# Attention and a two-stage mixer on one core: transfers turn q, k and x, more seven-product pairs, V's products on quarter row tiles

## The chip, the cores and the metric

The kernel runs on one core of a Trainium2 chip. TensorE (PE in the profile) multiplies, VectorE (DVE), ScalarE (ACT) and GpSimd (POOL) work on elements, SyncE (SP) only issues transfers, as POOL does too; 16 DMA engines carry them. The metric is the device time of one execution in microseconds; lower is better.

## What is computed

```python
def attention(q, k, v):                       # 4 x 8 heads x 768 x 64, n_global 8, n_local 96
    scores = q @ k.T / 8                      # a key is kept if it is one of the first 8,
    scores += -slope[h] * distance            # or lies 0 to 95 places behind the query
    return softmax(where(keep, scores, -1e9)) @ v
def mixer(x):                                 # x: 4 x 768 x 512, the heads side by side
    u = x + (x.T @ U @ V).T                   # U 768 x 32, V 32 x 768: low rank over the sequence
    return u + maximum(u @ w_ch1, 0) @ w_ch2  # 512 -> 2048 -> 512
```

The matrix products take fp16 and add in fp32.

## The kernel before, in words

**Pairs.** The 4 batches x 8 heads are handled as 16 pairs of heads, numbered 0 to 15; pairs 4b to 4b+3 are batch b. For each pair POOL loads q, k and v (`lq`, `lk`, `lv`), casting them to fp16; SP loads q and k of pair 0. The head size has to be on the partitions for q times k, so PE turns q and k by multiplying with the identity, six 128 x 128 pieces a turn for pairs from 4 on (`TQ`, `TK`, L611), and ACT or DVE copies the result out of PSUM (`EQ`, `EK`). `KO` builds a shifted copy of k whose first 32 keys are the global ones, `VC` and `VG` the same for v. `S` forms the scores (L734, 64 rows of the array a head, so two products run side by side), `EX` takes the exponential on ACT, `MK` multiplies by the mask, `PV` multiplies with v (L866, L867), and `RC` and `NM` divide and write x in fp32.

**The low rank.** `XC` casts x to fp16. `UP` sends six pieces of it through PE twice: times the identity, which leaves x turned in PSUM (L840), and times U (L845). `XE` copies the 32 columns of x U out, four times side by side, `XU` turns them (L948), `TE` copies them to `tmp`, and `HM` multiplies with V (L966) on top of the turned x in PSUM: the result is u turned. `HM` has two products of 384 columns; where `HR` says R, they take 64 rows each (32 with numbers and 32 of zeros, half a `vs` tile) and run side by side, for pairs 1, 8 and 12 they take all 128 rows. `E0` copies u from PSUM to `uT`, mostly on ACT.

**First layer of the mixer**, per batch: 16 tiles of 128 columns of w_ch1. A plain tile is `M1` (L1020, L1044: eight products of 384 columns) and a ReLU on ACT. Two tiles, j and j + 8, can instead be formed together by seven block products (Winograd's form of Strassen's scheme): `ZP1` to `ZP7` (L1115), each two products of 384 columns, 14 in place of 16. `ZT` forms the sums of u for it, `ZS` those of the weights; ACT keeps three partial sums (`ZU`, `ZW`, `ZX`), DVE adds them to PSUM (`ZA`, `ZB`, `ZD`, L1133), and separate ReLU passes follow over the results (`ZQ`, `ZV`, L1172, L1174). 14 pairs of tiles are done so: four each in batches 1 and 2, six in batch 3.

**Second layer**, per batch three units t, each 128 + 128 rows of the output, again by seven products `P1` to `P7` of eight products of 256 columns (L1246), with sums formed by `PA` and `PB`. `RS` adds the low-rank part through V (L1238, four products of 256 columns, 64 rows each), `DA` to `DH` add PSUM onto x, and `O` stores.

**The order.** `ORDER` lists some 1,000 tasks by short names, and a planner in the program assigns buffers and PSUM banks from booked durations and due times. Each engine then runs its tasks strictly in the list's order; each waits by semaphore for what it needs. A batch's attention is woven between the products of the batch before. q and k have three staging buffers, v four, turned q and k three each, x in fp16 three.

Of the kernel before, what the change touches and what calls it, by code (L numbers as in the profile page):

```python
# [10 lines left out]
FP32 = mybir.dt.float32  # L11
FP16 = mybir.dt.float16
# [9 lines left out]
wz iota lk1 lk0 lq0 vz relf bias1 rel3 bias0 lq1 lk3 bias2 bias4 Ck0.1 ones0 lv0 Ck0.0 SB0.2 vs1 mask1 Cq0.0 Cq0.1  # L22
SB0.0 TK0 lk2 EK0.0 EK0.1 KO0.1 lq2 KO0.0 TQ0 EQ0.0 lq3 EQ0.1 mask2 SB0.1 ones1 TK1 EK1 back S0.0 S0.2 S0.1 lv1 TQ1
EQ1 KO1 VC0 VG0 ones2 ones3 lk4 EX0.0 EX0.1 u16 TK3 EK3 EX0.2 SB1.1 SB1.2 S1.2 EX1.2 S1.1 EX1.1 vs0 PV0 RC0 NM0 XC0
KO3 lv2 TK2 EK2 KO2 VC1 VG1 lk5 SB2.1 TQ2 EQ2 SB1.0 S1.0 EX1.0 lv3 SB2.2 lq4 lq5 TQ3 S2.2 EX2.2 EQ3 S2.1 mixl PV1
SB3.1 S3.1 RC1 NM1 UP0 XE0 XC1 w1_1 EX2.1 w1_5 SB2.0 EX3.1 S2.0 XU0 TE0 VC2 SB3.0 TK4 EK4 VG2 HM0 S3.0 TK5 EK5 VC3
VG3 EX2.0 E00 SB3.2 w1_7 S3.2 w1_6 PV2 RC2 NM2 UP1 XC2 EX3.0 TQ4 EX3.2 lk7 PV3.0 PV3.1 PV3.2 RC3.2 XE1 XU1 RC3.0
NH3.0 RC3.1 NH3.1 lq7 NH3.2 NM3 EQ4 KO4 TE1 TQ5 EQ5 UP2 XE2 HM1 E01 UP3.0 XU2 TE2 UP3.1 UP3.2 XE3 HM2 E02 XU3 TE3
M1a0.3 M1c0.3 HM3 E03 vs2 E13 KO5 S4.1 lv4 EX4.1 mask0 EX4.2 M1d0.3 M1b0.3 RL0.3 M1a0.14 M1b0.14 w1_4 RL0.14 M1b0.15
lq6 M1b0.13 RM0.13 M1a0.2 M1c0.2 TK7 M1d0.2 MK4.1 RM0.15 w1_2 MK4.2 VC4 M1a0.13 VG4 RM0.14 EK7 KO7 RL0.13 M1b0.2  # L30
RL0.2 ZS6 w1_0 M1a0.15 S4.0 EX4.0 MK4.0 S5.0 w1_3 EX5.0 M1a0.10 mask3 TQ7 EQ7 lk6 mask5 M1a0.11 TQ6 EQ6 RL0.15
RL0.11 PV4 RC4 M1b0.4 RL0.10 lv5 M1b0.11 RM0.4 NM4 XC4 w2_2 w2_0 RM0.11 M1b0.12 S5.1 EX5.1 w2_3 ZS5 RM0.12 M1a0.6
M1b0.10 M1a0.12 EX5.2 w2_1 RM0.10 M1b0.7 RM0.7 TK6 EK6 KO6 M1a0.8 M1a0.0 RL0.6 ZS7 RL0.12 M1c0.0 M1d0.0 M1b0.0 RL0.0
lk8 MK5.0 MK5.1 VC5 TD0 VG5 MK5.2 PV5 M1a0.4 RL0.4 M1a0.7 PA0.3 PB0.3 UP4 XE4 RL0.7 M1a0.5 lq8 RL0.8 RC5 NM5 XC5
M1b0.5 RM0.5 M1b0.6 RM0.6 M1b0.8 RM0.8 RL0.5 XU4 TE4 TWa0 lk9 lv7 TWb0 PA0.1 PB0.1 M1a0.1 M1c0.1 M1d0.1 M1b0.1 RL0.1
PA0.0 PB0.0 M1b0.9 M1a0.9 S7.0 lk10 RM0.9 RL0.9 PA0.2 PB0.2 EX7.0 HM4 E04 RS0.0 P20.0 P10.0 DA0.0 lq9 mask7 TWa1
TWb1 S6.1 EX6.1 EX6.2 RS0.1 P10.1 P20.1 DA0.1 mask6 lv6 TQ8 P30.1 DF0.1 TK8 lq10 MK7.0 EQ8 UP5 XE5 VC7 P50.0 lq12
VG7 EK8 XU5 TE5 lk11 mask4 P30.0 DF0.0 S6.0 EX6.0 HM5 E05 MK6.2 P60.0 DB0.0 MK6.1 P60.1 DB0.1 S7.1 MK6.0 EX7.2 RS0.2
MK7.2 P10.2 DA0.2 P70.1 DD0.1 TQ10 lq11 EX7.1 MK7.1 TK9 EK9 KO9 ZS4 P70.0 lv11 TQ9 P20.2 EQ10 VC11 VC6 VG6 EQ9 TK10
EK10 KO10 DD0.0 P40.1 DG0.1 PV7 RC7 NM7 PV6 KO8 RC6 NM6 lv8 P60.2 P30.2 DC0.0 XC7 DB0.2 P50.1 DC0.1 XC6 UP7 UP6 XE7  # L40
DF0.2 P40.0 DG0.0 lv10 XE6 XU6 TE6 XU7 TE7 lv9 P70.2 DD0.2 HM6 E06 HM7 E07 S8.0 EX8.0 lq14 E17 ZP11.5 MK8.0 ZU1.5
P40.2 S8.1 EX8.2 EX8.1 TK11 EK11 ZT1 ZP11.4 ZU1.4 P50.2 M1a1.3 TQ11 M1b1.3 RL1.3 ZP21.5 ZP61.5 ZW1.5 O0.3 ZP21.4
DG0.2 KO11 EQ11 ZA1.5 ZA1.4 DC0.2 ZP61.4 ZW1.4 S9.1 EX9.1 MK8.1 ZP71.5 ZX1.5 M1a1.6 RL1.6 MK9.1 VC10 ZP71.4 ZX1.4
ZP51.5 ZB1.5 O0.4 M1a1.7 ZP51.4 VC9 EX9.2 ZB1.4 ZV1.4 ZP11.6 ZP31.5 ZP41.5 ZD1.5 ZR1.5 ZP41.4 ZP31.4 MK8.2 O0.2
ZD1.4 M1a1.2 M1b1.2 ZP11.7 ZR1.4 ZQ1.5 ZV1.5 ZQ1.4 PA1.2 O0.0 PB1.2 M1b1.6 ZU1.6 ZP61.6 RL1.7 ZU1.7 ZP21.7 ZA1.7
RL1.2 VC8 ZP61.7 ZW1.7 RM1.6 ZW1.6 M1a1.4 ZP21.6 ZA1.6 O0.5 VG8 PV8 ZP71.7 RL1.4 ZP71.6 ZX1.6 RC8 lk13 M1b1.7 RM1.7
O0.1 NM8 XC8 ZX1.7 PA1.1 S9.0 EX9.0 M1b1.5 M1b1.4 RM1.4 ZP51.6 ZB1.6 ZP41.6 RM1.5 UP8 XE8 MK9.0 ZP51.7 lk12 ZR1.6
TK12 EK12 TD1 ZP31.6 ZB1.7 M1a1.5 ZV1.7 ZD1.6 TQ12 RL1.5 XU8 EQ12 TE8 ZP41.7 ZR1.7 lv12 ZP31.7 ZD1.7 M1a1.0 M1b1.0
HM8 M1a1.1 M1b1.1 MK9.2 ZV1.6 RL1.0 ZQ1.6 ZQ1.7 PA1.3 PB1.1 E08 RL1.1 PA1.0 VG9 PV9 S10.1 RC9 RS1.1 P11.1 P21.1 lv14
P51.1 EX10.2 NM9 S10.0 PB1.3 PB1.0 DA1.1 EX10.1 XC9 S11.0 EX11.0 MK11.0 EX10.0 RS1.0 P21.0 P51.0 DC1.0 S11.1 EX11.2  # L50
P31.0 P11.0 MK10.1 P31.1 UP9 DF1.0 TQ14 VC12 EX11.1 DA1.0 P61.0 XE9 XU9 KO12 EQ14 TE9 MK11.2 MK11.1 VG11 PV11 lk14
TK14 lk15 EK14 DB1.0 P71.0 O1.0 DF1.1 P61.1 lq13 RC11 NM11 MK10.2 DD1.0 XC11 HM9 E09 S12.0 EX12.0 RS1.2 P11.2 P41.0
KO14 S12.1 EX12.1 DB1.1 P71.1 VG12 EX12.2 P31.2 DA1.2 MK10.0 VG10 DD1.1 PV10 MK12.0 TK13 EK13 P61.2 lq15 RC10 TQ13
EQ13 NM10 P21.2 XC10 KO13 UP10 lv13 UP11 XE10 DB1.2 P71.2 XU10 DF1.2 DC1.1 DG1.0 TE10 DD1.2 XE11 XU11 TE11 P41.1
DG1.1 VC14 O1.4 O1.3 HM10 E010 S14.0 EX14.0 HM11 E111 E011 MK12.1 MK14.0 P41.2 ZP12.7 ZU2.7 S14.1 EX14.2 ZT2 MK14.2
EX14.1 M1a2.5 ZP12.6 P51.2 DC1.2 M1a2.1 M1b2.1 TK15 EK15 KO15 ZU2.6 DG1.2 ZP62.6 RL2.5 ZP62.7 ZW2.6 M1b2.4 RL2.1
ZP72.6 ZX2.6 ZP52.6 ZB2.6 ZP12.4 RM2.4 M1a2.4 RL2.4 ZP22.7 ZA2.7 TQ15 EQ15 ZP32.6 ZD2.6 M1b2.5 ZP42.6 RM2.5 MK12.2
ZR2.6 M1a2.3 TD2 M1b2.3 PV12 ZP22.6 ZW2.7 ZP72.7 MK14.1 RL2.3 RC12 ZX2.7 ZP52.7 O1.2 M1a2.0 M1b2.0 O1.5 O1.1 NM12
XC12 ZB2.7 ZP32.7 ZU2.4 ZA2.6 ZQ2.6 ZV2.7 ZV2.6 VG14 PV14 RL2.0 ZD2.7 ZP62.4 ZP12.5 RC14 NM14 ZW2.4 ZP42.7 ZP22.4
ZA2.4 ZU2.5 ZR2.7 UP12 XE12 ZP72.4 PA2.0 ZX2.4 M1a2.7 ZP62.5 ZW2.5 ZP22.5 ZA2.5 XU12 TE12 ZP52.4 ZP42.4 RL2.7 ZP72.5  # L60
ZP52.5 HM12 M1a2.2 ZB2.4 ZX2.5 ZR2.4 ZB2.5 ZV2.5 M1b2.2 E012 ZP32.5 ZP42.5 ZR2.5 M1b2.7 RM2.7 XC14 UP14 XE14 ZP32.4
M1b2.6 ZQ2.7 PA2.3 ZD2.5 ZQ2.5 RL2.2 ZV2.4 ZD2.4 ZQ2.4 PA2.2 PB2.2 XU14 TE14 RM2.6 M1a2.6 RL2.6 PB2.0 PA2.1 RS2.1
HM14 E014 RS2.0 P12.0 DA2.0 P22.0 S13.1 EX13.1 EX13.2 P22.1 P12.1 P52.1 P62.0 S15.1 PB2.1 PB2.3 P32.0 EX15.2 MK13.1
DA2.1 DB2.0 P32.1 P62.1 P72.0 MK13.2 EX15.1 DF2.1 DF2.0 MK15.1 S13.0 EX13.0 lv15 S15.0 RS2.2 MK15.2 P52.2 P12.2
MK13.0 VG13 VC13 PV13 EX15.0 DB2.1 P72.1 MK15.0 DD2.0 VC15 RC13 VG15 PV15 DA2.2 NM13 RC15 P42.0 NM15 P62.2 ZS3.2
DD2.1 XC13 P22.2 UP13 XC15 UP15 DB2.2 P72.2 XE15 XU15 TE15 DG2.0 XE13 XU13 TE13 P32.2 DD2.2 HM13 HM15 E015 E115
DF2.2 ZS3.3 P52.0 P42.1 E013 ZP13.5 ZU3.5 M1a3.0 M1b3.0 ZT3 ZP13.2 RL3.0 DG2.1 DC2.1 O2.1 P42.2 ZP13.4 ZU3.2 ZP63.5
M1a3.1 ZU3.4 DC2.0 ZW3.5 ZP63.4 ZP73.5 DG2.2 ZW3.4 DC2.2 O2.5 ZX3.5 ZP63.2 ZP53.5 M1b3.1 ZB3.5 ZW3.2 RL3.1 ZP23.5
ZA3.5 ZP43.5 ZP73.4 ZV3.5 ZP23.4 ZA3.4 ZX3.4 ZP73.2 ZX3.2 ZP13.3 ZU3.3 TD3 ZR3.5 ZP53.4 ZB3.4 ZP33.5 ZD3.5 ZQ3.5
ZP43.4 ZR3.4 ZV3.4 ZP13.7 ZU3.7 ZP23.3 ZA3.3 ZP63.3 ZP33.4 ZD3.4 ZP53.2 ZB3.2 M1a3.5 ZW3.3 O2.3 ZQ3.4 PA3.2 RL3.5  # L70
O2.4 ZP43.2 ZR3.2 ZP23.2 ZA3.2 ZP13.6 ZU3.6 ZP53.3 ZP63.7 ZW3.7 ZP23.6 ZA3.6 ZP63.6 ZW3.6 ZP73.3 ZX3.3 ZP53.6 ZP73.7
ZX3.7 ZB3.3 ZP53.7 ZV3.2 ZB3.7 ZV3.7 ZP73.6 ZX3.6 ZP43.3 ZR3.3 ZP43.7 ZB3.6 M1b3.4 RM3.4 ZP33.7 ZD3.7 ZP43.6 ZP33.6
ZP33.2 ZD3.6 ZR3.6 ZV3.6 ZQ3.6 ZP33.3 ZR3.7 ZD3.3 ZV3.3 O2.0 M1a3.4 RL3.4 M1b3.5 RM3.5 ZP23.7 ZD3.2 ZA3.7 ZQ3.7
PA3.3 RS3.1 RS3.0 RS3.2 P23.2 ZQ3.3 ZQ3.2 PA3.1 P23.0 P23.1 P13.0 P13.2 PA3.0 PB3.0 P53.1 DA3.0 DA3.2 P13.1 P63.2
P53.0 PB3.3 O2.2 DA3.1 P63.0 DB3.2 PB3.2 P63.1 P53.2 PB3.1 P33.0 DB3.0 P73.0 DC3.1 DB3.1 P33.1 DF3.2 DC3.0 P33.2
O3.2a DC3.2 DF3.1 P73.1 O3.1 P73.2 DH3.2 O3.2 DD3.0 P43.0 DF3.0 O3.0 DD3.1 P43.1 DD3.2 P43.2a P43.2b O3.5a DG3.0
# [9 lines left out]
class Task:  # L86
    def __init__(self, name, eng, dur, fn, deps=(), lat=0.1, acq=(), rel=(), size=0.0, parts=1, mode=0, bw=(), br=(), fast=0):
        self.name, self.eng, self.dur, self.fn = name, eng, dur, fn
        self.deps = [d for d in deps if d is not None]
        self.lat, self.fast = lat, fast  # L90
        self.acq, self.rel, self.size, self.parts, self.mode = acq, rel, size, parts, mode
        self.start = self.end = None

        self.bw, self.br = bw, tuple(br) + tuple(g for g in rel if g.kind == "ps" and eng != PE)
# [11 lines left out]
class Planner:  # L106


    LANES = 8

    def __init__(self, counts, dma_rate, switch):
        self.tasks, self.names = [], {}
# [147 lines left out]
def kernel(  # L260
# [13 lines left out]
    nc = tc.nc  # L274
# [1124 lines left out]
```

## Time and profile before

| | |
|---|---|
| Time, median of 3 runs (lowest, highest) | 225.12 us (224.36, 225.25) |
| Span of the profiled execution, first to last instruction | 223.0 us |
| What lies around it, median less span | 2.1 us |
| PE busy, of the span | 216.4 us, 97% |
| DVE, ACT, POOL busy | 181.6, 147.0, 73.7 us |
| Products on PE (matmul instructions) | 2,424 |
| SP's transfers, issue (least, median, most) and landing | 0.585, 0.616, 2.116 us for the vo copies; 2.5 us to landing for 124 KB |

The profiled execution's own time is the span and about 2.1 us around it. "Busy" on PE counts a product from its start to its modelled end; products overlap, so the price of one in a row of products is the distance between starts. In the chain of waits a piece such as "0.34 PE ps L611 x6" is six products that took 0.34 us of PE's queue.

### The profile page before, as it was taken

Reading aid. Unit: us, or ns where it says so; the run is one execution under the profiler, and the core shown is the slowest. Engines: PE = TensorE matmul, PEld = TensorE weight load, DVE = VectorE, ACT = ScalarE, POOL = GpSimd, SP = SyncE. Lnnn points to the kernel's source line nnn. Section 1 sums busy time; section 2 is a strip of 40 time slices with the busy share of each in tenths; the row PEclk is TensorE's granted clock in tenths of the full one; section 3 lists DMA queues with packets and bytes.
Section 4 is the critical chain, followed back from the end, with each engine's and each line's share of the span. In section 5 each row is a group of like instructions: output and inputs, shape, how many; then the busy total and the mean of one; then the engine's idle time right before and its main releaser. Section 6 shows DMA issues by size and latency. Waiting matters only on the chain.

```text
span 223.0 us, 5965 instructions
## 1 busy us (share of the span) xinstructions
PE 216.4 (97%) x2424; PEld 158.5 (71%) x2424; DVE 181.6 (81%) x403; ACT 147.0 (66%) x260; POOL 73.7 (33%) x97
## 2 busy tenths in 40 slices
PE   8799899999999999999999999999999999999994
PEld 3466656675879976666888876666788875658883
DVE  5688966999987987888978688597978796889872
ACT  7888798768858669788757557787742458782000
POOL 8989959714894940010851000011000000000000
PEclk9999999999999999999999999999999999999999
DMA  6999999999999997662997021409100006000025
GB/s 173 178 170 149 159 161 185 184 206 166 158 157 92 140 191 141 224 46 37 68 116 98 18 79 65 132 4 71 33 0 3 0 3 259 25 1 3 0 97 190
DMA packets 87404, 23.31 MB, mean 104 GB/s; under 512 B 73840, under 2 KB 84784, under 8 KB 87376
## 3 DMA queue, kind: packets, MB, share of 16 engines
q0 software_dynamic: 72880, 13.74, 75.6%
q1 hardware_dynamic: 14496, 9.19, 14.2%
q8 instruction: 19, 0.31, 0.6%
q14 instruction: 9, 0.07, 0.1%
HBM read 27.56 MB, written 6.29 MB: 152 GB/s over the span
## 4 chain that ended last, share of the span: by engine, by line
PE 84%; DMA 7%; POOL 5%; issue 2%; DVE 1%; ACT 0%; DVEq 0%; POOLq 0%
PE ps L1246 34%; PE ps L1115 14%; PE ps L1020 11%; PE ps L1044 7%; PE ps L734 4%; DMA vt<-in_v_dram 4%; PE ps L611 3%; DMA stgq<-in_q_dram 3%; PE ps L840 2%; PE ps L867 2%; PE ps L866 2%; POOL stgq L457 1%; POOL w L507 1%; PE ps L1238 1%; PE ps L966 1%
## 5 line engine op out<-in xcount | busy, mean ns | idle before, releaser
L799 ACT ACTIVATE ep<-ps 128x1024 f16<-128x1024 f32 (+1 forms) x48 | 44.0, 952 | 16.3 <-PE ps L734 15.1
L1246 PEld LDWEIGHTS <-htr 128*128 128x128 f16 x392 | 36.2, 98 | 6.1 <-issue 1.9
L1020 PE MATMUL ps<-uT,w 128*128 128x384 f16 x176 | 33.3, 326 | 0.0
L1258 DVE TENSOR_TENSOR x_sb<-x_sb,ps 128x256 f32<-128x256 f32 (+1 forms) x60 | 26.8, 463 | 7.6 <-PE ps L1246 7.2
L1246 PEld LDWEIGHTS <-sA 128*128 128x128 f16 x288 | 27.4, 98 | 4.2 <-issue 0.7
L461 POOL DMA_DIRECT2D vt<-in_v_dram x16 | 16.7, 1047 | 32.9 <-PE ps L867 29.7
L1026 ACT ACTIVATE htr<-ps 128x384 f16<-128x384 f32 x44 | 20.7, 493 | 5.6 <-PE ps L1020 5.3
L1246 PE MATMUL ps<-w,sA 128*128 128x256 f16 x192 | 24.2, 273 | 0.0
L1246 PE MATMUL ps<-tB,htr 128*128 128x256 f16 (+1 forms) x200 | 24.2, 268 | 0.0
L1020 PEld LDWEIGHTS <-w 128*128 128x128 f16 x176 | 16.5, 98 | 10.6
L1246 PE MATMUL ps<-w,htr 128*128 128x256 f16 x192 | 23.5, 273 | 0.0
L457 POOL DMA_DIRECT2D stgq<-in_q_dram x24 | 19.9, 852 | 5.4 <-PE ps L611 3.3
L1044 PE MATMUL ps<-uT,w 128*128 128x384 f16 x112 | 21.3, 326 | 0.0
L457 POOL DMA_DIRECT2D stgk<-in_k_dram x24 | 20.0, 852 | 2.6 <-DMA w<-in_moe_w_ch_dram 1.0
L1133 DVE TENSOR_TENSOR htr<-ps,zu 128x384 f16<-128x384 f32 x30 | 16.4, 553 | 4.7 <-PE ps L1115 3.0
L362 ACT ACTIVATE zu<-ps 128x384 f32<-128x384 f32 x30 | 14.7, 493 | 5.7 <-PE ps L1115 5.3
L812 DVE TENSOR_TENSOR ep<-ep,mask 128x1024 f16<-128x1024 f16 x24 | 16.2, 684 | 1.4 <-ACT ep L799 0.9
L905 DVE TENSOR_TENSOR x_sb<-ps,rcp 128x768 f32<-128x768 f32 x16 | 15.3, 956 | 0.9 <-DMA vo<-vt 0.4
L1044 PEld LDWEIGHTS <-w 128*128 128x128 f16 x112 | 10.7, 98 | 6.6
L1115 PEld LDWEIGHTS <-w 128*128 128x128 f16 x108 | 10.2, 98 | 6.1
L734 PE MATMUL ps<-qT,kT 64*128 64x128 f16 x192 | 14.0, 217 | 0.4 <-DVE kT L364 0.4
L1115 PE MATMUL ps<-uT,w 128*128 128x384 f16 x56 | 13.4, 326 | 0.0
(124 smaller groups left out, 450.0 us busy)
## 6 DMA issues: line engine op xcount, KB each, us to landing
out_dram<-x_sb SPq DMA_DIRECT2D x20, 256.0 KB, 2.2
vt<-in_v_dram POOLq DMA_DIRECT2D x16, 192.0 KB, 5.9
stgk<-in_k_dram POOLq DMA_DIRECT2D x24, 96.0 KB, 6.6
stgq<-in_q_dram POOLq DMA_DIRECT2D x24, 96.0 KB, 5.6
w<-in_moe_w_ch_dram POOLq DMA_DIRECT2D x8, 256.0 KB, 7.1
w<-in_moe_w_ch_dram POOLq DMA_DIRECT2D x4, 512.0 KB, 11.7
vo<-vt SPq DMA_DIRECT2D x8, 123.8 KB, 2.5
out_dram<-x_sb SPq DMA_DIRECT2D x7, 128.0 KB, 2.2
```

The lines of the kernel that those rows point to most:

```text
L457: nc.gpsimd.dma_start(o[:, i], src[b, h0 + i].rearrange("(n p) d -> p n d", p=P))
L461: nc.gpsimd.dma_start(vt[gv.slot][:, :, :, 0:D], v[b, h0:h0 + 2].rearrange("h (n p) d -> p h n d", p=P),)
L734: nc.tensor.matmul(t[:, hi, j * P:(j + 1) * P], lhs, qt[r, i * P:(i + 1) * P], start=not biased, stop=True, skip_group_check=biased,)
L799: nc.scalar.activation(ep[gep.slot][:, :, lo:512], ps[:, gsc.slot:gsc.slot + 2, lo:512], AF.Exp, scale=qk_scale)
L812: nc.vector.tensor_tensor(ev, ev, mv, ALU.mult)
L1020: nc.tensor.matmul(ps[:, g.slot, 0:HS], w1[:, dc, jt * P:(jt + 1) * P], ub[:, dc, i * HS:(i + 1) * HS], start=(dc == 0), stop=(dc == NDC - 1),
L1026: nc.scalar.activation(htr[:, jt, i * HS:(i + 1) * HS], ps[:, g.slot, 0:HS], AF.Relu)
L1044: nc.tensor.matmul(ps[:, g.slot + half, 0:HS], w1[:, dc, jt * P:(jt + 1) * P], ub[:, dc, half * HS:(half + 1) * HS], start=(dc == flat[0]) ...
L1115: nc.tensor.matmul(bank(g), a()[:, i], bq[:, i], start=first and i == 0, stop=last and i == 1, skip_group_check=True,)
L1133: return lambda: nc.vector.tensor_tensor(o, x(), y(), ALU.add)
L1246: nc.tensor.matmul(o if part is None else o[:, part], a[:, j, c0 + cols.start:c0 + cols.stop], bq[:, j] if part is None else bq[:, j, part ...
L1258: nc.vector.tensor_tensor(o, o, x, ALU.add)
```

## The change

Its edits, with what the compiled program has before and after:

- q and k of pairs 8 to 15 are turned by a transposing transfer issued from SP, in place of `T` on PE and `E` on ACT or DVE: 16 transfers; 96 products fewer.
- x of pairs 4 to 15 is turned by such a transfer into `uT` (`XT`): 12 transfers, 72 products fewer. PSUM then holds only the low-rank part, and `E0` becomes an addition of PSUM onto `uT`, always on DVE.
- V is loaded twice, into 32 + 32 partitions of each half. `HM` uses 32 rows a product; for pairs 4 and 5, 6 and 7, up to 14 and 15, one `HM` does both, four products of 384 columns on four quarters of the rows. `RS` uses 32 rows a product too (two at a time, as before).
- Batch 2 has six seven-product pairs, so 16 in all. Their weight sums are made for two neighbouring pairs by one instruction of double width.
- The ReLU of these pairs goes into DVE's addition, as one custom instruction (add, then clamp to 0 and 3e38); the 28 separate passes (19 on DVE, 9 on ACT) go.
- `PA`, `PB` are cut into their single instructions `Sa` to `Sd`, each with its own due time.
- `ORDER` is a new list. POOL's first transfer comes ahead of its small set-up work, all loads of pairs 0 to 3 come ahead of those of pairs 4 and 5, and PE's list has 89 changes between row tilings (128 rows, 64, 32, and the 64-column form) in place of 73.

PE goes from 2,424 products to 2,248, SP from 64 rows to 85, DVE from 403 to 378, ACT from 259 to 241.

```diff
-    "Z": ((1, (4, 5, 6, 7)), (2, (4, 5, 6, 7)), (3, (2, 3, 4, 5, 6, 7))),
+    "Z": ((1, (4, 5, 6, 7)), (2, (2, 3, 4, 5, 6, 7)), (3, (2, 3, 4, 5, 6, 7))),
+    "XD": [4, 5, 6, 7, 8, 9, 10, 11, 12, 13, 14, 15],
+    "QD": [8, 9, 10, 11, 12, 13, 14, 15],
+    "H2": (4, 6, 8, 10, 12, 14),
+    "R2": {0: (), 1: (), 2: (), 3: ()},
...
         def arrange(x, stg, gs, ld, gt, dst, i):
+            if p in CFG["QD"]:
+                def turn():
+                    o = dst().rearrange("c (n p) -> c n p", n=NB)
+                    nc.sync.dma_start_transpose(o, stg[gs.slot].rearrange("p a b -> p (a b)"))
+                return [add(SP, TSP, turn, ld, acq=[gt], rel=[gs], size=TSZ, lead=1.25, name=f"E{x}{p}")]
...
                 for c in cs:
+                    if not turned:
+                        nc.tensor.matmul(
+                            ps[:, gx.slot + c // 3, (c % 3) * P:(c % 3 + 1) * P], xx[:, c], ident16,
+                            start=(c % 3 == 0), stop=False, skip_group_check=True,
+                        )
                     nc.tensor.matmul(
+                        ps[:, gx.slot, 384:384 + R], xx[:, c], u16[:, c],
+                        start=turned and c == 0, stop=(c == NB - 1), skip_group_check=True,
                     )
...
+                def xturn():
+                    o = uT[b % 2][:, hp].rearrange("p (n c) -> p n c", n=NB)
+                    nc.sync.dma_start_transpose(o, x16[gx16.slot].rearrange("p n c -> p (n c)"))
...
+        def hmix(k=0, gx=gx):
             for half in (0, 1):
-                r = slice(64 * half, 64 * half + 64) if hrow else slice(0, P)
+                r = slice(64 * half + R * k, 64 * half + R * (k + 1))
                 nc.tensor.matmul(
                     ps[:, gx.slot + half, 0:HS], tmp[b % 2][r, hp * P:(hp + 1) * P], vs[r, half],
-                    start=False, stop=True, skip_group_check=True,
+                    start=turned, stop=True, skip_group_check=True,
                 )
+            def hboth(other=other, hmix=hmix):
+                other(0)
+                hmix(1)
...
+                    if turned:
+                        nc.vector.tensor_tensor(o, o, i, ALU.add)
+                    else:
+                        copy(e, o, i)
...
             def tt(o, x, y):
-                return lambda: nc.vector.tensor_tensor(o, x(), y(), ALU.add)
+                return lambda: nc.vector._custom_dve(TENSOR_ADD_SAT, out=o, in0=x(), in1=y(), s0=3.0e38, s1=0.0)
...
-                    r = slice(VR[n], VR[n] + 64)
-                    nc.tensor.matmul(o, vs[r, n, cols], m[r], start=first_, stop=False, skip_group_check=True)
+                        r = slice(VR[n] + k * R, VR[n] + (k + 1) * R)
+                        yield half(g, i), vs[r, n, cols], m[r], i == 0
```

## The prediction, as it was put on record

> **What bounds the kernel now.** I read the busy shares and the slices first:
>
> ```profile
> span 223.0 us, 5965 instructions
> ...
> PE 216.4 (97%) x2424; PEld 158.5 (71%) x2424; DVE 181.6 (81%) x403; ACT 147.0 (66%) x260; POOL 73.7 (33%) x97
> ...
> PE   8799899999999999999999999999999999999994
> ...
> PEclk9999999999999999999999999999999999999999
> DMA  6999999999999997662997021409100006000025
> ```
>
> PE is busy for 97% at the full granted clock, and its free time lies in the first six slices and the last. Busy time can hide waits, so the stages come next (start:end, then busy us of PE, PEld, DVE, ACT, POOL):
>
> ```profile
> 8.00:24.00 16.00, 14.85 (x279) 9.84 (x276) 14.19 (x31) 13.35 (x16) 15.03 (x22) 1.00 2.15 165
> ...
> 60.00:141.00 81.00, 81.00 (x966) 62.65 (x964) 67.14 (x139) 58.50 (x102) 26.70 (x31) 1.00 1.02 110
> ...
> 179.00:200.50 21.50, 21.50 (x142) 13.53 (x142) 18.18 (x41) 16.14 (x35) 0.00 (x0) 1.00 0.20 75
> ```
>
> From 60 to 141 us PE has no gap at all, while DVE is at 83% and ACT at 72%. The chain of waits agrees: up to 36.6 us it runs over POOL's issues and the loads (8.09 us are one load of v), from there to 219.8 us over PE almost alone, and about 3 us of DVE and the last store follow. So a product taken off PE after 36.6 us shortens the kernel by its place in PE's queue, as long as nothing else comes late. Prices are therefore distances between starts (start, length, what):
>
> ```profile
> 60.02 0.34 PE ps L611 x6
> ```
>
> ```profile
> 99.79 0.22 PE L840 MATMUL ps<-ident,x 128*128 128x128 f16 x1
> ...
> 100.25 0.18 PE L845 MATMUL ps<-u,x 128*128 128x32 f16 x1
> 100.28 0.49 PE L1115 MATMUL ps<-zt,w 128*128 128x384 f16 x2
> ```
>
> ```profile
> 28.87 0.34 PE L966 MATMUL ps<-vs,tmp 64*128 64x384 f16 x2
> 29.05 0.22 PE L734 MATMUL ps<-qT,kO 64*128 64x128 f16 x2
> ```
>
> ```profile
> 106.48 0.19 PE L866 MATMUL ps<-vo,ep 128*128 128x65 f16 x1
> 106.51 0.19 PE L867 MATMUL ps<-vt,ep 128*128 128x65 f16 x1
> 106.64 0.23 PE L734 MATMUL ps<-qT,kO 64*128 64x128 f16 x2
> ```
>
> A turn of q or k takes 0.335 us of the queue (0.33 or 0.34 in the chain). One `UP` takes 0.49 us. An `HM` on half-row tiles takes 0.18 us. A narrow product takes 0.03 us (106.48 to 106.51), and the change of row tiling behind it 0.13 in its place, 0.10 more.
>
> **The parts, one by one.** All act on PE's queue if not said otherwise.
>
> 1. *Turns of q and k*, pairs 8 to 15. All 16 stand in the chain between 60.0 and 141.0 us, where PE has no gap: 16 x 0.335 = 5.36 us go. Their 16 copies out of PSUM go too.
> 2. *Turns of x*, 12 pairs, all after 60 us. Six narrow products stay. The trace has none of 32 columns by themselves: at the 0.03 us of the 65-column row they take 0.18 us, at the 0.06 us of a 128-column piece 0.36. I take 0.18, the nearer in width: 12 x (0.49 - 0.18) = 3.72 us go (at the other end 1.56).
> 3. *Two more seven-product pairs*: 2 x 2 products of 384 columns less; four such take 0.65 us in the chain ("0.65 PE ps L1020 x4"): 0.65 us go.
> 4. *`HM` on quarters.* For pairs 4 to 15 there are ten at 0.18 and two on all rows at 0.33 (104.25 to 104.58 us): 2.46 us. Six double ones replace them. The trace has no quarter tiles. If the four run together as the two halves do, six take 1.08; if two by two, 2.16. I take the first, since the half-row row shows tiles side by side at the length of one: 1.38 us go (0.30 at the other end). Pair 1 gains another 0.15. `RS` keeps two products side by side: nothing.
> 5. *Changes of row tiling*, 73 before and 89 after: 16 x 0.10 = 1.60 us come. `RS` and `HM` no longer share their tiling with `S`; at 107.10 us an `RS` still follows `S` without such a gap. The Trainium skill ("TensorEngine Tiling (Array Packing)", Key Properties) has this rule against the change: a change of tiling mode drains the array, a change of tile does not. The trace agrees, with that 0.10 us; without the rule the sum would be 1.6 us lower.
> 6. *DVE.* Fifteen additions onto `uT` come (9 x 0.956 and 6 x 0.553 us, by the PSUM rows of that width: 11.9) and six sums of the new pairs (3.3); 19 ReLU passes (6.0), six copies of u (4.5), three of q and k (2.0), four of `tmp` (1.1), three casts of x (1.8), the vs memset (0.5) and about 1.9 of weight sums go; one copy of k comes (0.6). Net -2.0. ACT, in the same way, loses about 16 us. The custom addition has no row. It reads and writes what the 0.553 us row does, so I take that; ends 0.49 (ACT's pass of that size) and 0.956 (double length). At 0.956 the 48 of them cost DVE 19 us and bring it to 199 of 214: then it is late inside batches 2 and 3. At nothing, PE is the cover.
> 7. *The transposing transfers.* 28 come on SP, 192 KB each; no such transfer is in the trace. Nearest are SP's copies inside SBUF: 0.62 us to issue, landing after 1.9 to 9.2 us, the median 2.4 for v and 3.9 for k's 120 KB. I take 0.62 and 3.9. By "DMA: Bandwidth & Descriptors" of the Trainium skill, its latency table, transposing runs at 261 GB/s, which would be an estimate of 0.75 us for one; no run here shows that, and the sum does not use it. q and k are loaded well ahead, and 3.9 us is covered there by other pairs' work in PE's list. POOL's loads gain: staging is freed by a transfer and not by PE. Where the cover is thin is the start of batches 1, 2 and 3. There `UP`, `XE`, `XU`, `TE` ran before the turned x was needed and still do, but the double `HM` waits for the second pair, and two DVE additions follow (0.956 each, where ACT took 0.81 each and side by side with DVE's); all that before the first `ZP1`, with three to six `P` and `S` tasks as cover. I put 0.7 us on each start, nearly one such addition: 2.0 us come. Ends: 0 and 6 (two more additions' length each).
> 8. *The opening.* Before, the last load of batch 0 (v of pair 3) is issued at 15.89 us, behind four loads of 96 KB for pairs 4 and 5; now it is behind none. 384 KB at the 165 GB/s of 8 to 24 us is 2.3 us. But ACT is busy 13.4 and DVE 14.2 of those 16 us, so I count 1.0 us gained (ends: 0.5 lost, as POOL's iota now stands behind a load issue of 0.75, and 2.3).
>
> The end, `P` of batch 3 at full PE and the last store, stays.
>
> Sum: -5.36 - 3.72 - 0.65 - 1.38 - 0.15 + 1.60 + 2.0 - 1.0 = -8.7 us. Span 223.0 to 214.3. The profiled execution has 223.0 in its span and the median of the runs is 225.1, 2.1 more; keeping that, 225.1 - 8.7 = **216.4 us**. With every low end: -5.36 - 3.72 - 0.65 - 1.38 - 0.15 + 1.6 - 2.3 = -12.0, and 213; without the drain 211.5. With every high end: -5.36 - 1.56 - 0.65 - 0.30 - 0.15 + 1.6 + 6 + 0.5 = 0, and 225.
>
> **Rivals.**
>
> *The sum is right and more comes* (0.12): covers hold at every batch start and the opening gains its 2.3 us: 211.5 to 213.5. For it: ACT is relieved by 16 us. Against: DVE would stand at 85% of the span.
>
> *x comes late at every batch start* (0.15). If a transfer lands after 3.9 us but two or more in SP's queue follow one another rather than overlap, the last x of a batch lands after about 8 us; the chain to `HM` is some 2 us (two PSUM copies of 0.28 and four short waits), cover on PE some 3. Each start then waits 3 us: 9 in place of 2, and 223.4 us, still a little faster. For it: the vo copies' longest landing is 9.2 us. Against: SP's issues stand 0.6 us apart and land 2.4 us later, so they do overlap.
>
> *SP becomes the bound, and the kernel slower* (0.13). SP issues strictly in order. From about 75 to 175 us its list now holds 28 turns and about 38 other transfers at 0.62 us, 23.6 us. That leaves 76 us for 28 turns, 2.7 us each. If a turn keeps SP or the engines longer than that, q of pairs 8 and on comes later each time. At 3.1 us the whole gain of 8.7 is gone; that is the point from which it decides. At 3.9 us (k's landing, nothing overlapping) SP needs 109 + 24 = 133 us for the 100: 216 + 33 = 249 us. For it: DMA slices stand at 9 up to 84 us and a turn might move in small pieces. Against: the overlap just named, and the low DMA shares after 117 us.
>
> **How the numbers follow.** Forecast 0.60, its own range 213 to 221. More comes 0.12, late x 0.15, SP 0.13. The range 211.5 to 225 leaves out SP's 0.13 and some 0.04 besides. Half a per cent, about what a measurement of this kernel can tell from no change, is 224.0 to 226.2 us. Faster: 0.60 + 0.12 and 0.10 of late x = 0.82. Same: 0.05 of it. Slower: 0.13.
>
> **What would show it.** PE products 2,248 and PE busy near 206 us. The chain should run over PE from about 35 us on, with SP's transfers in it for under 5 us. `UP` should take about 0.18 us, a double `HM` about 0.18, and the custom addition 0.55. Wrong would be: long PE waits on transfers of kT, qT or uT (late x, or SP); DVE above 90% in the batches 2 and 3; a transposing transfer that keeps SP for over 2.7 us. If PE's busy time falls as said and the span does not, part 7 failed; if PE's busy time does not fall, parts 2 and 4.

## The result, and the profile after

The changed kernel takes 227.12 us (median of 20 runs, 225.06 to 229.41) against 224.93 us for the kernel before (20 runs, 223.70 to 226.64). The ratio is 1.0078, with a 95% interval of 1.0055 to 1.0102; it leaves out the four executions that lie over 1.5% above the fastest of the changed kernel, and the other 16 have a median of 226.7 us. That is slower by 0.8%, or some 1.8 us, where 216.4 us was forecast. The profiled execution is one of the longest, 229.0 us with a span of 227.2 and a mean granted clock of 0.977, so what follows shows the loss larger than it usually is; over the 20 executions that clock lies between 0.977 and 0.992.

The busy shares and slices of the profile page after the change:

```profile
span 227.2 us, 5608 instructions
...
PE 210.2 (92%) x2248; PEld 149.7 (66%) x2248; DVE 175.7 (77%) x378; ACT 129.4 (57%) x242; POOL 74.8 (33%) x99
...
PE   6998999999999839999999966999999999999994
...
PEclk9999999999999967999999997999999999999999
DMA  7999999999999999993996995972062615000034
```

PE's row had no digit below 7 between its ends before; now it has two holes, at 3 (the fifteenth slice, 80 to 85 us) and at 66 (131 to 142 us). The clock row dips at each hole or behind it. By stages (start:end, then busy us of PE, PEld, DVE, ACT, POOL, then the granted clock):

```profile
60.00:78.00 18.00, 17.55 (x217) 14.59 (x215) 14.51 (x30) 5.86 (x14) 8.00 (x10) 1.00 1.91 141
78.00:89.00 11.00, 6.27 (x60) 4.01 (x58) 5.01 (x11) 3.05 (x4) 7.96 (x9) 0.69 1.97 143
89.00:120.00 31.00, 31.00 (x305) 21.27 (x303) 28.70 (x59) 23.85 (x46) 8.60 (x10) 1.00 1.26 150
...
132.00:144.00 12.00, 7.65 (x57) 4.22 (x56) 5.05 (x11) 4.59 (x7) 0.00 (x0) 0.86 1.05 124
144.00:184.00 40.00, 40.00 (x444) 29.41 (x443) 37.49 (x79) 23.02 (x45) 0.82 (x1) 1.00 0.49 86
```

Outside the two holes these stages are full, but for 0.45 us of the first. PE's list of waits names what opened them (engine, line, what it waited for; us in total, times, the longest):

```profile
PE ps L771 <- DVE uT L1055: 5.0, 2, 4.7
PE ps L1187 <- DVE uT L1043: 4.1, 1, 4.1
PE ps L1393 <- POOL vt L470: 2.2, 1, 2.2
```

L771 is `S`, L1187 `ZP`; L1055 and L1043 are `E0`, the addition of PSUM onto the turned x. The third wait is that of the first products of all (part 8 below). The chain of waits shows what `E0` itself waited for:

```profile
63.15 0.14 PE ps L882 x6
...
65.32 7.45 DMA kT<-stgk
72.77 9.50 DMA uT<-x
...
82.39 0.97 DVE uT L1055
...
83.41 1.51 PE ps L771 x22
84.91 1.82 PE ps L1306 x8
```

The turn of x of pair 6 was issued at 72.77 us and landed 9.50 us later. Until then `E0` cannot add, so the low-rank part keeps its PSUM banks, and `S` of pair 9, next in PE's list, gets none. The last line shows the aftermath: eight products of `P` take 1.82 us, where eight took 0.87 to 0.98 elsewhere in the same chain.

Part of the lateness came before the transfer. The cast of x of pair 6 ends at 69.80 us (ACT, 68.96 + 0.84), but SP was still issuing the turns ahead of it in its list (start, time of the issue):

```profile
65.32 3.26 SPq L656 DMA_TRANSPOSE kT<-stgk  x1
68.68 2.27 SPq L978 DMA_TRANSPOSE uT<-x  x1
71.07 1.61 SPq L656 DMA_TRANSPOSE qT<-stgq  x1
72.77 3.82 SPq L978 DMA_TRANSPOSE uT<-x  x1
```

So 3.0 us of the 12.5 from cast to landing were spent in SP's queue. The second hole is pair 11's, and there the product that waits, `ZP`, reads u itself:

```profile
120.00 0.95 DVE uT L1055
...
121.42 0.86 DVE uT L1055
...
127.06 0.92 DVE x L409
...
129.31 8.11 DMA uT<-x
```

Ahead of this turn the chain runs over DVE from 120.00 us on, two of the new additions in it, to the cast of x at 127.06: here the cast was late too. No run takes that part by itself.

Now the clock, in slices of 4 us:

```profile
80.00:84.00 4.00, 0.59 (x13) 0.59 (x14) 1.60 (x3) 0.05 (x1) 4.00 (x6) 0.67 1.72 122
84.00:88.00 4.00, 4.00 (x29) 2.19 (x26) 2.44 (x7) 2.69 (x3) 3.62 (x4) 0.50 2.26 144
88.00:92.00 4.00, 4.00 (x38) 2.55 (x38) 3.86 (x9) 3.31 (x5) 0.00 (x0) 0.98 1.78 236
```

From 84 to 88 us PE is busy all the time and does 29 products at clock 0.50. So a stop is paid twice: as idle time, and as half the clock behind it.

**The account**, on spans. The clock is at half from 81.34 to 88.17 us, where PE is busy from 83.41 on, and from 139.36 to 142.78: 8.2 busy us, of which 4.1 are stretch. At full clock PE would be busy for 210.2 - 4.1 = 206.1 us, 10.3 less than before. Idle time rose from 223.0 - 216.4 = 6.6 to 227.2 - 210.2 = 17.0 us, by 10.4: 8.8 in the two stops, 1.3 more at the first products, and little else. Together -10.3 + 10.4 + 4.1 = +4.2, the difference of the spans.

### The profile page after: what moved, and what is told of

The parts are those of the page before. It is cut to its first block, busy times and chain, and to the rows that moved or that the text cites. A ratio compares the mean times of both kernels' runs of the same rounds, so it can differ in the third digit from the quotient of the medians.

```text
span 227.2 us, 5608 instructions
## 1 busy us (share of the span) xinstructions
PE 210.2 (92%) x2248; PEld 149.7 (66%) x2248; DVE 175.7 (77%) x378; ACT 129.4 (57%) x242; POOL 74.8 (33%) x99
## 4 chain that ended last, share of the span: by engine, by line
PE 61%; DMA 26%; DVE 7%; POOL 3%; issue 1%; POOLq 0%; DVEq 0%
PE ps L1306 23%; PE ps L1187 16%; DMA vt<-in_v_dram 10%; DMA uT<-x 8%; PE ps L1093 7%; PE ps L1117 6%; DMA kT<-stgk 3%; PE ps L771 3%; DMA vo<-vt 3%; DMA stgk<-in_k_dram 2%; DVE x_sb L937 1%; PE ps L899 1%; DVE uT L1055 1%; PE ps L898 1%; PE ps L1393 1%
## 5 line engine op out<-in xcount | busy, mean ns | idle before, releaser
L1093 PE MATMUL ps<-uT,w 128*128 128x384 f16 x160 | 31.3, 331 | 0.0
L1204 DVE CUSTOM_DVE_ANT_0 htr<-ps,zu 128x384 f16<-128x384 f32 x36 | 19.2, 552 | 7.9 <-PE ps L1187 6.2
L1306 PE MATMUL ps<-w,sA 128*128 128x256 f16 x192 | 23.6, 273 | 0.0
L407 ACT ACTIVATE zu<-ps 128x384 f32<-128x384 f32 x36 | 17.1, 492 | 9.5 <-PE ps L1187 9.0
L1093 PEld LDWEIGHTS <-w 128*128 128x128 f16 x160 | 15.5, 99 | 9.8 <-issue 0.3
L1187 PEld LDWEIGHTS <-w 128*128 128x128 f16 x128 | 12.2, 98 | 12.1 <-issue 4.6
L1117 PE MATMUL ps<-uT,w 128*128 128x384 f16 x96 | 19.9, 341 | 0.0
L771 PE MATMUL ps<-qT,kT 64*128 64x128 f16 x192 | 15.0, 225 | 4.9 <-DVE uT L1055 4.7
L1099 ACT ACTIVATE htr<-ps 128x384 f16<-128x384 f32 x40 | 18.4, 508 | 1.5 <-PE ps L1093 1.2
L1187 PE MATMUL ps<-uT,w 128*128 128x384 f16 x64 | 13.9, 331 | 4.1 <-DVE uT L1043 4.1
L771 PEld LDWEIGHTS <-kT 64*128 64x128 f16 x192 | 9.6, 97 | 8.9 <-issue 8.5
```

The costliest lines, as they stand in the source:

```text
L407: nc.scalar.activation(dst, src, AF.Copy)
L771: nc.tensor.matmul(t[:, hi, j * P:(j + 1) * P], lhs, qt[r, i * P:(i + 1) * P], start=not biased, stop=True, skip_group_check=biased,)
L1093: nc.tensor.matmul(ps[:, g.slot, 0:HS], w1[:, dc, jt * P:(jt + 1) * P], ub[:, dc, i * HS:(i + 1) * HS], start=(dc == 0), stop=(dc == NDC - 1),
L1099: nc.scalar.activation(htr[:, jt, i * HS:(i + 1) * HS], ps[:, g.slot, 0:HS], AF.Relu)
L1117: nc.tensor.matmul(ps[:, g.slot + half, 0:HS], w1[:, dc, jt * P:(jt + 1) * P], ub[:, dc, half * HS:(half + 1) * HS], start=(dc == flat[0]) ...
L1187: nc.tensor.matmul(bank(g), a()[:, i], bq[:, i], start=first and i == 0, stop=last and i == 1, skip_group_check=True,)
```

## The experiments

Each ratio is to the kernel before, run beside it on the same chip, with its 95% interval. Theory A: the turns of x land late and PE waits for them. Theory B: the turns of q and k in front of them in SP's queue do it. In the diffs, the names taken out of `ORDER` or moved in it are those of the edited tasks; nothing else is in another place, except where said.

**1. x of batch 1 back on PE.**

```diff
-    "XD": [4, 5, 6, 7, 8, 9, 10, 11, 12, 13, 14, 15],
+    "XD": [8, 9, 10, 11, 12, 13, 14, 15],
```

> Batch 1's x (pairs 4 to 7) is turned on PE again and copied out of PSUM as before; the 8 transfers of x for batches 2 and 3 and all 16 of q and k stay. Theory A (the last turned x of batch 1 lands late, 82.3 us, PE stands for about 4.7 us and then runs at half clock for about 6): that stop and that slow stretch go, 4.7 + 3.4 us, against 4 x 0.31 us of products that come back; about 219 to 221 us, PE stop near 135 us unchanged, granted clock about 0.99. Theory B (SP's queue is simply too full with q and k as well): E of q and k still come late, PE stands elsewhere before 100 us; 224 us or more.

Measured: 220.8 us, ratio 0.983 (0.975 to 0.991). The windows over both holes of the changed kernel, now in this one:

```profile
78.00:89.00 11.00, 11.00 (x104) 7.12 (x102) 8.87 (x20) 9.84 (x16) 6.27 (x7) 1.00 1.82 158
...
132.00:144.00 12.00, 12.00 (x88) 7.18 (x87) 9.77 (x23) 10.37 (x21) 0.00 (x0) 1.00 0.70 191
```

The first hole is gone, and the second, expected unchanged, moved ahead and shrank to one wait of 2.0 us, as its turn landed after 6.14 us; the clock is full throughout. The span falls by 9.3 us to 217.9: idle time by 6.2, clock stretch by 4.1, and PE's full-clock work rises by 1.0. Undoing four of the 28 turns takes back more than the loss. Theory A holds.

**2. q and k of pairs 8 and 9 back on PE**, x left on transfers; their `T` tasks were put next to their `E` tasks.

```diff
-    "QD": [8, 9, 10, 11, 12, 13, 14, 15],
+    "QD": [10, 11, 12, 13, 14, 15],
```

> q and k of pairs 8 and 9 alone are turned on PE again, so 4 transfers fewer stand between the x turns of batch 1 on SP; all x turns stay. Theory A in its plain form (a turn beside loads is slow by itself): x of pair 6 still lands some 7 us after its issue but is issued as soon as it is cast; the stop of PE shrinks by 1 to 2 us only; 224 to 226 us. Theory B (the q and k turns ahead of it in SP's queue hold it up, 1.2 to 3.3 us each): x of pair 6 is issued 3 us earlier or more, the stop shrinks below 2 us and the clock holds; 219 to 221 us with 4 x 0.34 us of products back.

Measured: 222.8 us, 0.990 (0.985 to 0.994). The landings of x have a median of 3.2 us in place of 5.0, the longest 6.9 in place of 9.5; from 70 to 90 us PE is busy for 18.4 of 20 us and the clock is full. PE's longest waits behind that of the first products:

```profile
PE ps L1188 <- DVE uT L1044: 1.5, 1, 1.5
PE ps L883 <- ACT x L408: 0.8, 1, 0.8
PE ps L772 <- DVE x_sb L1319: 0.7, 1, 0.7
```

The first of them lies at 131 us, in the second hole. The 1.6 us that PE is idle from 70 to 90 us are the other two and 0.2 us for an `E0` at 72; none waits for a turned x to land. So without the turns of q and k x of batch 1 comes in time: B holds for the first hole. It does not part their place in the queue from their traffic: from 70 to 76 us the DMA engines moved 73 GB/s here and 148 in the changed kernel. That is what the next run is for.

**3. The order on SP alone**: the turns of k and q of pairs 8 and 9 (with their `KO`) behind `XT6`.

```diff
-EK9 ... EQ8 ... EK8 ... KO8 ... KO9 ... EQ9 ... XT6
+... XT6 EK8 EQ8 KO8 EK9 EQ9 KO9
```

> All transfers stay; in SP's list the turns of q and k of pairs 8 and 9 come behind the last x turns of batch 1 instead of between them (S of pair 8 waits longer in exchange). Theory B (SP's order): x of pair 6 is issued 2 to 3 us earlier and lands by 77 to 79 us, the first stop nearly goes; 221 to 223 us if q and k, now late, cost little. Theory A (the transfer is slow beside the loads whatever its place): x lands some 7 us after its issue still, the stop shrinks by 2 us at most, and S of pairs 8 and 9 adds a stop; 225 us or more.

Measured: 228.4 us, 1.017 (1.010 to 1.025). The first hole is smaller (17.6 of 20 us busy, clock 0.91), the second larger (19.8 of 25 us from 120 to 145 us, clock 0.86; its stop is 4.6 us). In the first hole PE now waits for ACT (1.28 us) and DVE (1.09 us), and for no turned x: with all transfers kept, their order alone takes that wait away, so the queue is a cause there. What was put behind came late in turn, as the chain to the wait of 1.09 us shows:

```profile
74.69 2.77 DMA kT<-stgk
...
78.13 0.33 DVE x_sb L1318
...
78.50 0.32 PE ps L771 x5
```

In time, order alone gains nothing.

This trace also shows what lowers the clock. After those two waits, with 0.5 us of products between them, it was at half from 79.47 to 82.89 us, and after the second hole from 134.09 to 140.91. Each stretch of half clock, here and in the changed kernel, is 3.41 us long or twice that, and the starts lie 17 x 3.41 us apart there and 16 x 3.41 here. In the 3.41 us ahead of the four starts PE was busy for 0.75, 0.77, 1.47 and 0.58 us. So what seems to count is how full fixed windows of 3.41 us are, not the length of one stop; four falls in two executions show it, and no run was made for it. One such window is 0.0075 of the mean clock, so the 0.992, 0.985 and 0.977 of the 20 executions are one, two and three of them.

**4. The clock: zero products as cover.** First try: 20 products of zeros, 384 columns each, ahead of the two waiting tasks, onto the PSUM bank of pair 6 or 11.

```diff
+FILL = {"S9.0": (6, 20), "ZP12.2": (11, 20)}
...
+            if t.name in FILL:
+                p, n = FILL[t.name]
+                for _ in range(n):
+                    nc.tensor.matmul(ps[:, gxs[p].slot, 0:HS], ..., start=False, stop=True)
```

> All of the change stays; 20 products of zeros (384 columns, 3.3 us at full clock) are added on PE in each of the two stops, onto a PSUM bank that waits there anyway. They add zero to the result. If the half clock after each stop is a consequence of the stop itself, the clock stays at 1.00 and the time falls by up to 5 us, to 221 to 224 us, while the waits for the turned x stay. If the clock falls for another reason, the time stays at 226 to 228 us.

Measured: 231.0 us, 1.024 (1.016 to 1.033). The edit missed its aim: the zeros had to wait for `E0` too, and ran behind the stop:

```profile
78.79 1.04 PE L1308 MATMUL ps<-tB,htr 128*128 128x256 f16 x8
82.92 3.47 PE L1414 MATMUL ps<-zero 128*128 128x384 f16 x20 [3.08 <-DVE uT L1057]
```

The bracket gives the idle time ahead. It still tells something: behind this stop of 3.08 us the zeros run at full clock, while the stops of 4.7 and 4.1 us halved it. (That is the profiled execution; in two of the four the mean clock fell to 0.978 and 0.983.) Second try: 30 zero products of 256 columns right behind the last product before each stop, onto that product's own bank.

```diff
+FILL = {"P70.1": 30, "P41.2": 30}
```

> All of the change stays. 30 products of zeros of 256 columns (3.2 us) follow directly on the last product ahead of each stop, onto the PSUM bank that this product wrote; they add zero. In e3 the zeros had waited with the rest and ran behind the stop; here they run inside it, so PE stands some 1.5 us rather than 4 to 5. If the half clock is a consequence of a stop of PE of over about 4 us: granted clock 1.00, and 4 to 5 us less than the changed kernel, 221 to 224 us, because the turned x lands no earlier. If the clock is not set by the stop: 226 to 228 us and a clock below 1.00.

Measured: 225.2 us, 1.000 (0.997 to 1.004), against 1.0078 (1.0055 to 1.0102). The page's clock row and the stage of the first hole:

```profile
PEclk9999999999999999999999999999999999999999
```

```profile
70.00:90.00 20.00, 17.92 (x188) 13.71 (x187) 12.20 (x26) 8.04 (x15) 9.60 (x11) 1.00 1.86 145
```

The turn of the first hole lands as late as before (8.20 us in the chain), 2.1 us of idle time stay, and the clock never falls. The half clock is thus a consequence of the stop and not of the new products. Keeping the clock up gives back 0.7%, or 1.6 us. I had expected 4 to 5. The stretch of the profiled execution is 4.1 us, and at the 0.985 that is usual in the 20 executions it is at most 3.4. And the zeros of the second stop cost time themselves: `E0` had ended at 134.90 us, but they kept PE until `ZP` began at 136.34.

**5. x only by transfer in batch 3**, where POOL loads nothing.

```diff
-    "XD": [4, 5, 6, 7, 8, 9, 10, 11, 12, 13, 14, 15],
+    "XD": [12, 13, 14, 15],
```

> x of batches 1 and 2 (pairs 4 to 11) is turned on PE again, only batch 3's x and all of q and k by transfers. Theory A: both stops go; 8 x 0.31 = 2.5 us of products come back; 9 us of stops and 5 us of half clock go: 213 to 217 us. If DVE's additions onto the turned x or the full SP queue were to blame rather than the late landing, stops stay near 80 and 135 us: 221 us or more.

Measured: 217.8 us, 0.971 (0.964 to 0.977). **The opening**, on top of this: the zero memset and the iota ahead of POOL's first load of pair 1.

```diff
-lk0 lq0 lk1 wz ones3 iota
+lk0 lq0 wz iota lk1 ones3
```

> e4 (x of batches 1 and 2 on PE) with one more edit undone: POOL's zero tile and iota come ahead of its first load again. If the late first product (2.23 us in the changed kernel, 0.89 before) costs at the end, 1 us less than e4's 217.8: 216.5 to 217. If the opening is set by the loads and by ACT, as the equal start of the first layer (28.1 us in both) suggests: 217.8 within 0.3, or up to 0.7 more because the first load is issued later.

Measured: 217.45 us, 0.966 (0.961 to 0.972): the best version, but its interval overlaps that of the one without the opening. Its page:

```profile
span 215.5 us, 5699 instructions
...
PE 208.9 (97%) x2304; PEld 151.0 (70%) x2304; DVE 173.4 (80%) x373; ACT 132.5 (62%) x247; POOL 74.9 (35%) x99
...
PE   8899899999999999999999999999999999999993
```

Idle time is 6.6 us, the same as in the kernel before. What PE does less (216.4 - 208.9 = 7.5) is exactly what the span is shorter. No run has x of batch 3 on PE as well, so what its four turns bring is not measured by itself. The next experiments start from this version, called the best one.

**6. Some turns of x in batches 1 and 2 again**: pairs 4, 5, 8, 9, and then 4 and 5 alone.

```diff
-    "XD": [12, 13, 14, 15],
+    "XD": [4, 5, 8, 9, 12, 13, 14, 15],
```

> e7 with x of pairs 4, 5, 8 and 9 turned by transfers again: the first two of batches 1 and 2, whose turn has the rest of the attention as cover; only the late ones 6, 7, 10 and 11 stay on PE. If it is only the late transfers that stop PE: 4 x 0.31 = 1.2 us less than e7's 217.45, 216 to 216.8. If any transfer of x beside the loads delays what stands behind it in SP's queue, or DVE's additions onto the turned x (0.96 us each) hold up batch 2: 217.5 to 221.

Measured: 220.2 us, 0.982 (0.979 to 0.986).

```diff
+    "XD": [4, 5, 12, 13, 14, 15],
```

> e10 with x of pairs 8 and 9 on PE too, so that batch 2 has no turned x at all and batch 1 only its first two. Between e7 and e10 if each early transfer saves its 0.31 us: 216.8. If e10 loses by batch 2 (where DVE had no free time from 120 to 128 us in the changed kernel), this one is faster than e10 and than e7.

Measured: 220.95 us, 0.984 (0.981 to 0.987). Both are slower than the best version, with intervals that do not meet. Neither has a hole: their longest waits on PE are 1.3 and 1.6 us, and PE is busy for 208.8 and 209.2 us, as in the best version. What grew is the sum of small waits, 9.4 and 8.5 us of idle time in place of 6.6. Which of them the two early turns cause is not settled. Taking 8 and 9 out again did not help, so nothing shows that the loss lies in batch 2.

**7. The double `HM` undone** in the best version: one `HM` a pair.

```diff
-    "H2": (4, 6, 8, 10, 12, 14),
+    "H2": (),
```

> e7 (x of batches 1 and 2 on PE, POOL's set-up first) with one HM for each pair again instead of one for two; every product still takes 32 rows, two side by side. The prediction's price: six double HMs at 0.18 us against twelve single ones at 0.18, 1.1 us, and six more changes of row tiling each way at 0.10, about 1.2: 2 us slower than e7's 217.45, some 219.5, if PE's queue decides. If the wait for the second pair costs as much as the products save: within 0.5 us of e7, or faster.

Measured: 218.2 us, 0.972 (0.970 to 0.974); PE 209.8 us busy, 0.9 more than with the double one, and the span 0.9 longer. The expected 2 us had six more changes of row tiling each way in it; the trace has 91 changes with and without the double one, so the 0.9 us are the products alone.

**8. q and k on PE again**: all 16 turns (without the opening), and then those of pairs 8 and 9 in the best version. The `T` tasks stand next to their `E` tasks; the rest of the order was not planned anew.

```diff
-    "QD": [8, 9, 10, 11, 12, 13, 14, 15],
+    "QD": [],
```

> e4 with all 16 turns of q and k on PE too, so that only batch 3's four x turns are transfers. If turning q and k by transfers brings its place in PE's queue, this is 16 x 0.335 = 5.4 us slower than e4: 222 to 224 us. If those turns cost in waits about what they save (POOL waits 17.6 and 10.0 us for staging in e4), it is within 1.5 us of e4.

Measured: 235.6 us, 1.048 (1.039 to 1.057). PE is busy for 216.6 us, 7.7 more than without the edit (5.4 was the price), and idle for 15.9.

```diff
+    "QD": [10, 11, 12, 13, 14, 15],
```

> e7 with q and k of pairs 8 and 9 on PE, as in e2, on a kernel without the stops. If these four turns bring their place in PE's queue, 4 x 0.335 = 1.3 us slower than e7: 218.5 to 219. If they bring nothing because they hold staging buffers (POOL waits 13.5 and 9.4 us for them in e7) and the loads behind them come late: within 0.4 us of e7 or faster.

Measured: 221.1 us, 0.985 (0.982 to 0.987): PE busy +2.1 us, idle time +1.5 against the best version. Turning q and k by transfer pays, but how much is not clean here: in a strict order, a task put in brings waits of its own.

**9. Loads beside turns that had none.** In the best version the turns of x of batch 3 land after 2.7 to 2.8 us. POOL loads nothing there, but there are no turns of q and k beside them either. So six loads that nothing reads were added, first in the form of pairs from 4 on (pieces of 256 bytes), then in that of pairs 0 to 3 (1,536 bytes).

```diff
             t.fn()
+            if t.name == "XC14":
+                for i in range(6):
+                    o = (stgq, stgk)[i % 2][i // 2]...
+                    for h in range(2):
+                        nc.gpsimd.dma_start(o[:, h], (q, k)[i % 2][3, 6 + h]...)
```

> This is e7_x12_open with six loads added that nothing reads: after the cast of x of pair 14, POOL loads q and k of pair 15 three times more each, in the usual form of pairs from 4 on (packets of 256 bytes), into the q and k staging buffers that are free by then. They are issued at about 153.7 to 164 us, and so lie beside the four turns of x of batch 3, which in e7 were issued at 156 to 168 us with no load beside them and landed after 2.7, 2.8 and 2.8 us. Theory A (a turn lands late because of the loads beside it): the landings of these four rise to 5 us or more, the longest to 7 or more, and the time rises by 0.5 to 4 us over e7's 217.45. Rival (a turn lands late because of its place in SP's queue, behind the turns of q and k, whatever POOL loads): they stay at 2.7 to 3.2 us and the time at 217.5 +- 0.5.

> The same six loads beside the turns of x of batch 3 as in e13, of the same volume, but in the form that pairs 0 to 3 use, which reads pieces of 1,536 bytes in place of 256, one transfer a load. If what delays a turn is the number of small pieces that the loads put into the DMA engines, the landings stay below those of e13, at 3 to 4 us, and the time within 0.5 us of e7's 217.45. If it is the volume, they are as in e13. If loads delay nothing (the rival of e13), 2.7 to 3.2 us here too.

From the view of the line of `XT`, its issues and landings; the best version, with the short pieces, with the long ones:

```profile
L978 SPq DMA_TRANSPOSE uT<-x x4: 1211/1216/1278, 156.1 to 166.6; - x4
...
DMA to landing us min/median/max: 2.7/2.8/2.8
```

```profile
L978 SPq DMA_TRANSPOSE uT<-x x4: 1212/1216/1287, 156.9 to 167.3; - x4
...
DMA to landing us min/median/max: 3.4/5.1/6.5
```

```profile
L978 SPq DMA_TRANSPOSE uT<-x x4: 1211/1244/1427, 157.1 to 169.7; - x4
...
DMA to landing us min/median/max: 2.7/4.0/10.4
```

Same queue, same turns, only loads added: the median landing goes from 2.8 to 5.1 us. The loads are a cause, shown on four turns of one execution each. That the number of pieces does it is not: with long pieces one turn took 10.4 us. The times, 218.4 us (0.968, 0.964 to 0.972) and 218.7 us (0.970, 0.967 to 0.974), can't be told from the best version's.

## Why the prediction was wrong

**Part 7 failed**, the transposing transfers, as the prediction's last sentence had named it: PE's busy time fell as said, and the span did not. It took SP's copies inside SBUF as the nearest rows: 0.62 us to issue and 3.9 to land. The view of `XT` in the changed kernel:

```profile
L978 SPq DMA_TRANSPOSE uT<-x x12: 1212/1260/3819, 53.0 to 178.5; - x12
...
DMA to landing us min/median/max: 2.7/5.0/9.5
```

An issue is 1.21 us at the least, and the longest landing decides, not the median. Two things were missed besides. The three to six `P` and `S` tasks counted as cover were too little, and in batch 1 the `S` among them were none: `S` of pair 9 needs the PSUM that `E0` frees, so it stood still with the rest. And a stop was priced at its length, with nothing for the clock. Priced were 2.0 us, at most 6; the account shows 8.8 of idle time in the two stops and 4.1 of clock.

On that clock, the Trainium skill ("TensorE: Matmul & The Clock Gate", "Why this matters for your kernels") asks for no idle gaps on PE of more than about 3 us between bursts of products, since one window of idle brings half rate. The runs here agree on the single stops, full clock behind 3.08 us and 0.50 behind 4.1 and 4.7 us. Experiment 3 goes further: waits of 1.28 and 1.09 us close together were enough.

**Part 8 failed too**, in sign. The small set-up work behind POOL's load makes PE's first products wait 2.2 us; PE is busy for 55.8 of the first 60 us, 56.7 before. The first layer of batch 0 begins at 28.11 us, 28.13 before. With that work ahead again (experiment 5) it is 57.1 of 60, 0.4 more than before: what is left of the 1.0 said.

**Parts 1 to 5 were right as a sum.** They gave -11.26 us of products and 1.60 of gaps between tilings, -9.66 together; measured is -10.3 of PE's busy time at full clock, 206.1 us where "near 206" was said. The gaps were not measured by themselves. `UP` takes 0.14 us (chain above; 0.18 taken), 0.5 us more over 12 pairs. The double `HM` is worth 0.9 us of PE by experiment 7, where six `HM` at 0.18, 1.08, was the price.

**Part 6 held**: DVE fell by 5.9 us, more than the 2.0 said, ACT by 17.6 (16 said), and the custom addition, which no row had shown, takes 0.552 us (0.553 taken). From the page's costliest groups:

```profile
L1204 DVE CUSTOM_DVE_ANT_0 htr<-ps,zu 128x384 f16<-128x384 f32 x36 | 19.2, 552 | 7.9 <-PE ps L1187 6.2
```

**The rivals.** "x comes late at every batch start" was the mechanism: it gave 3 us a start and 223.4 us. It was two starts of three, 4.7 and 4.1 us each, and the clock on top took it past the time before. "SP becomes the bound" was not it as a whole: the median issue of 1.26 us is far below the 2.7 us from which it was to decide, and PE is full from 144 to 200 us. But single issues of 3.26 and 3.82 us are above it, and for the first stop SP's queue was a cause (experiments 2 and 3). The slower case should therefore have stood under late x, with no upper end at 225.

## What to carry to other kernels

Moving work from a full engine to transfers pays only if the longest landing beside other traffic is covered, by tasks that don't need the same buffers or PSUM banks: here the turns of x lost where loads ran (batches 1 and 2), and landed in 2.8 us where nothing was loaded (batch 3). Covering the longest is not always enough: x of pairs 4 and 5 made no hole and still lost. Waits on PE of 4 us cost more than their length, because the clock falls behind them. So take the worst landing of the nearest row, add the queue ahead of it, ask which bank is held until then, and try such a change stage by stage: 217.45 us, 3.4% under the kernel before, came from keeping all of this change but 8 of its 28 turns and the opening's order.

## What the runs showed of the hardware

- A transposing transfer of 192 KB lands 2.7 to 2.8 us after its issue where nothing else is moved, and up to 9.5 us after it beside POOL's loads and other turns (10.4 beside loads alone, experiment 9); its issue keeps SP for 1.21 us, up to 3.8 there, where a plain copy takes 0.62.
- Behind stops of 4.7 and 4.1 us PE ran at half the clock for 4.8 and 3.4 us; behind one of 3.08 us it did not, and behind two waits of 1.28 and 1.09 us close together it did, for 3.4 us. Half clock came in stretches of 3.41 us, each start behind 3.41 us in which PE was busy for 1.47 us or less.
- A product of 128 x 32 columns costs 0.023 us in a row of six (0.14 us). The custom addition with a clamp takes as long as a plain one.
